# First batch of an attention and MoE kernel: query-major products in plain float32

## The chip, the cores and the metric

The kernel runs on one core of one Trainium2 chip. The metric is the device time of one execution in microseconds, the median of several runs. The engines are TensorE (PE; its loading of weights is PEld), VectorE (DVE), ScalarE (ACT), GpSimd (POOL) and SyncE (SP), which issues the DMAs here.

## What is computed

Causal attention mixed with a read from a memory, for 4 batches, 8 heads, 576 positions and 64 columns per head, and behind it two feed-forward stages over the 2304 tokens.

```python
scores = scale * np.matmul(q, k.transpose(0, 1, 3, 2))      # causal mask, softmax
local = np.matmul(a, v)
q_p = phi(q)                                  # where(x > 0, x, exp(x) - 1) + 1
mem_ret = np.einsum('bhsd,bhde->bhse', q_p, M_prev)
mem_norm = np.einsum('bhsd,bhd->bhs', q_p, z_prev)[..., None] + 1e-06
out = g * (mem_ret / mem_norm) + (1 - g) * local            # g = sigmoid(beta) per head
...
r = np.maximum(x @ w_in, 0.0); y = (s * (r * r) + b) @ w_out
z = (sigmoid(y @ w_gate) * (y @ w_val)) @ w_out2
```

## The kernel before

Nearly all products are split products: each float32 operand is rounded to the engine's shorter format (`F32R`) as a high half, the difference is the low half, and three products (high by high, low by high, high by low) are summed. So most tiles are written twice, by ScalarE the high half, by VectorE or GpSimd the low half.

**Stage one** is attention together with h, the product with `w_in`. Attention goes by pairs of heads, 16 pairs, four to a batch (`jobs`, line 356). For a pair, `plan_prep` loads and transposes k and q (tiles `KT`, `QT`) and makes phi(q), which is divided by its own norm on GpSimd (`phi_z`, `phi_s`, `phi_n`, lines 530 to 554), transposed (`ft`) and stacked as two halves (`FS`, line 429). The values and `M_prev` are split on GpSimd (`VHL`, `mst`). `plan_scores` has the scores with the queries on the partitions, in five tiles of 128 rows (the last holds 64 rows of both heads). VectorE takes the mask and the minimum (line 606), ScalarE the exponential with the row sum (line 668), VectorE 1/sum with 1 - g in it (line 676), and GpSimd divides P (`norm`, line 684). `plan_products` transposes P in 25 blocks of 128 x 128, splits them on the way out of PSUM (`p_hi`, `p_lo`, lines 776 and 780), and multiplies with the values as the stationary operand (lines 806 and 807) and the memory's part behind it (line 810): the result `acc` has the head's columns on the partitions and up to 320 queries along. It goes to `XB` (lines 830, 834), and when all four pairs of a batch are there, the batch's two windows, of 256 and 320 queries, are split into x (lines 891, 895). A group of h (`h_mm`, line 319) is 12 products of 256 or 320 columns: it needs the whole window of x and one of 16 tiles of `w_in`, which are made from float64 words on ScalarE, VectorE and GpSimd (lines 250 to 271).

**Later stages.** y, the product with `w_out` (line 1057), in 96 steps of 12 products, reads relu(h) back from DRAM. Then come the gated products in seven half-size products each (line 1294, tiles `m` and `set`) and the last product (line 1397), in three rounds. At the start of the first round, `w_out2` is made on the same engines.

**What sets the order.** Every piece of work is a task of `Plan` with an engine, a cost, a due time, what it reads and writes, and the buffers it takes. `Plan.order` goes through time and lets each engine that is free take the most urgent task that is ready. The tasks then stand in that order in each engine's queue, which runs in order. The due times come from the table `TUNE` (for instance `u + AT["pt"]` with u = 100 for each pair). Buffers that matter here: `s`, four PSUM banks; `VHL`, `QT`, `KT`, `mst` two each; `PTA`, `PTB` one.

```python
    chunks = [
        (*w, f + i) for f in range(0, NF, 2) for w in windows if w[0] == 0 for i in range(2)
    ]
    chunks += [(*w, f) for w in windows if w[0] for f in range(NF)]
```

The h groups of the first batch come first, two tiles of `w_in` at a time over both windows, then those of the other batches.

Of the kernel before, what the change touches and what calls it, by code (L numbers as in the profile page):

```python
# [150 lines left out]
def attention_moe_kernel(  # L151
# [18 lines left out]
    P = 128  # L170
# [192 lines left out]

    def load_consts2():
        for e in range(2):
            c = slice(e * NQ, e * NQ + NT4)
            nc.vector.tensor_copy(iom[:, :, c], iomg[:, e::2].unsqueeze(2).broadcast_to([P, NP, NT4]))
            r = slice(e * LAST, (e + 1) * LAST)
            nc.vector.tensor_copy(iom[r, :, NT4], iomg[r, e::2])

    def load_raw(j, src, dst, ta):
        b, p, t0, t1 = jobs[j]
        te = min(t1, NQ - 1)
        d4 = dst.rearrange("p t (h d) -> p t h d", h=2)
        for e in range(2):
            nc.sync.dma_start(
                d4[:, ta:te, e],
                src[b, 2 * p + e, ta * P : te * P].rearrange("(t p) d -> p t d", p=P),
            )
        if t1 == NQ and src is q:  # L380
            for e in range(2):
                nc.sync.dma_start(
                    d4[e * LAST : (e + 1) * LAST, NQ - 1, e], src[b, 2 * p + e, (NQ - 1) * P :]
                )
        elif t1 == NQ:
            lo = 0 if src is k else P - LAST
            nc.sync.dma_start(
                d4[lo : lo + LAST, NQ - 1],
                src[b, 2 * p : 2 * p + 2, (NQ - 1) * P :].rearrange("h p d -> p h d"),
            )  # L390

    def load_mem(j):
        b, p = jobs[j][:2]
        h = slice(2 * p, 2 * p + 2)
        raw = T["mraw", j] = at.tile([P, 2, D], F32, tag="mraw", name=f"mraw{j}", bufs=1)
        for i in range(2):
            nc.sync.dma_start(raw[i * D : (i + 1) * D], M_prev[b, h].rearrange("h d e -> d h e"))
        z = T["z", j] = at.tile([P, 2, D], F32, tag="zbc", name=f"zbc{j}", bufs=1)
# [20 lines left out]
    def bank(nt):  # L419
        return "s" if nt <= 4 else "w"  # L420
# [6 lines left out]
    def stack_lo(t, ds):  # L427
# [9 lines left out]
        "PTC": 1, "XB": 1, "x0": 1, f"x{SPLIT}": 1, "raw": 2, "f": FB, "wt": 16,  # L437
# [31 lines left out]
    def plan_prep(j):
# [276 lines left out]
    def plan_products(j):  # L746
# [138 lines left out]
        for win, (c0, n) in enumerate(((0, SPLIT), (SPLIT, BW))):  # L885
            if p == NP - 1 and (t0 == 0 if win == 0 else t1 == NQ):
# [26 lines left out]
    def plan_h(m):  # L913
# [619 lines left out]
```

## Time and profile before

| what | value |
|---|---|
| runs | 1090.73 us median of 3 (1089.75 to 1091.71) |
| profiled execution, its span | 1090.0 us (the page gives no other time of it; the median stands 0.7 us above) |
| busy shares | PE 95%, PEld 90%, DVE 70%, ACT 59%, POOL 55% |
| matrix products | 6496 |
| DMA | 145.95 MB, 134 GB/s mean |

The busy shares are averages over the whole span. The page also cuts the span into 40 slices; in those of the first 100 us TensorE's digits are lower than later and its granted clock is below full, and VectorE's are at 8 and 9. The rows below read that stretch, the stage behind it and one later stretch apart from each other.

### The profile page before, as it was taken

What the parts mean: (1) busy time and instruction counts of PE and PEld (TensorE: products, weight loads), DVE (VectorE), ACT (ScalarE), POOL (GpSimd) and SP (SyncE); (2) the same over time, 40 slices, a digit from 0 to 9 for tenths busy, and PEclk for the clock granted to TensorE, in tenths of its full rate; (3) what the DMA queues carried; (4) which work ended last, traced back from release to release, by engine and by line L of the source; (5) the groups of instructions that cost most, each with busy time, mean ns of one, the idle gap of its engine ahead of it and who ended that gap; (6) DMA issues with size and microseconds to landing.
All of it is one profiled execution on the core that took longest, in us unless ns stands there. A gap on an engine that the chain in (4) does not pass through costs nothing.

```text
span 1090.0 us, 18804 instructions
## 1 busy us (share of the span) xinstructions
PE 1040.3 (95%) x6496; PEld 977.0 (90%) x6496; DVE 766.3 (70%) x1434; ACT 647.6 (59%) x1407; POOL 598.4 (55%) x590
## 2 busy tenths in 40 slices
PE   4887998999999998999999999899999999999998
PEld 3676997899999998999999999898789998899986
DVE  5998987867667645777897765999726677266631
ACT  4877787787778656566666654565335453245421
POOL 5656666545434415474784554999427774177600
PEclk8877999999999999999999999999999999999999
DMA  5333554232323118868577776544214330133100
GB/s 135 80 82 81 170 145 120 72 85 81 106 85 92 47 61 264 259 204 267 174 245 262 261 268 221 183 160 160 87 63 136 113 125 29 63 119 118 69 24 35
DMA packets 135600, 145.95 MB, mean 134 GB/s; under 512 B 68176, under 2 KB 123472, under 8 KB 135504
## 3 DMA queue, kind: packets, MB, share of 16 engines
q1 hardware_dynamic: 135072, 144.74, 41.6%
q8 instruction: 51, 0.84, 0.3%
q14 instruction: 45, 0.37, 0.1%
q10 hardware_dynamic: 432, 0.01, 0.0%
HBM read 106.96 MB, written 37.75 MB: 133 GB/s over the span
## 4 chain that ended last, share of the span: by engine, by line
PE 80%; DVE 7%; POOL 7%; issue 2%; ACT 2%; DMA 1%; SPq 0%; DVEq 0%; POOLq 0%; ACTq 0%
PE m L1294 17%; PE h L319 17%; PE y L1057 16%; PE o L1397 14%; PE sc L626 3%; PE acc L806 3%; PE acc L807 2%; DVE set L1306 2%; PE pt_B L753 1%; PE sc L652 1%; POOL ws L1278 1%; POOL p L1316 1%; PE acc L810 1%; POOL w_out L271 1%; POOL P L684 1%
## 5 line engine op out<-in xcount | busy, mean ns | idle before, releaser
L1294 PE MATMUL m<-yt,ws 128*128 128x384 f32 x1512 | 264.5, 335 | 4.9 <-POOL ws L1278 3.5
L1294 PEld LDWEIGHTS m<-yt,ws 128*128 128x128 f32 x1512 | 262.0, 188 | 7.2 <-POOL ws L1278 4.7
L319 PE MATMUL h<-x,w_in 128*128 128x256 f32 (+1 forms) x1536 | 224.6, 300 | 5.5 <-POOL w_in L271 2.0
L319 PEld LDWEIGHTS h<-x,w_in 128*128 128x128 f32 x1536 | 207.8, 189 | 11.5 <-issue 3.7
L1306 DVE TENSOR_TENSOR set<-m,set 128x384 f32<-128x384 f32 x252 | 133.7, 554 | 57.8 <-PE m L1294 55.3
L1278 POOL TENSOR_TENSOR ws<-wf,ws 128x512 fp32r<-128x512 f32 (+1 forms) x108 | 124.7, 1175 | 86.4 <-ACT ws L1270 86.4
L1032 POOL TENSOR_SCALAR rr<-rr,sb_s,sb_b 128x384 f32<-128x384 f32 x96 | 103.8, 1088 | 96.7 <-ACT rr L1028 92.9
L1397 PE MATMUL o<-w_out,ps 128*128 128x512 f32 x648 | 154.0, 399 | 1.9 <-DVE ps L1387 1.5
L1397 PEld LDWEIGHTS o<-w_out,ps 128*128 128x128 f32 x648 | 122.7, 190 | 32.4 <-DVE ps L1387 2.3
L1057 PE MATMUL y<-gh,w_out 128*128 128x384 f32 x768 | 149.1, 335 | 2.4 <-ACT gh L1038 1.0
L1270 ACT CAST ws<-wf 128x512 fp32r<-128x512 f32 (+1 forms) x144 | 81.6, 568 | 103.4 <-PE m L1294 68.9
L1057 PEld LDWEIGHTS y<-gh,w_out 128*128 128x128 f32 x768 | 134.3, 188 | 3.3 <-ACT gh L1038 1.3
L1316 POOL TENSOR_TENSOR p<-set,set 128x384 f32<-128x384 f32 x72 | 85.7, 1214 | 40.9 <-DVE set L1306 40.9
L684 POOL TENSOR_SCALAR P<-P,rs 128x384 f32<-128x384 f32 (+3 forms) x144 | 85.2, 612 | 38.9 <-DVE rs L676 18.4
L1043 DVE TENSOR_TENSOR gl<-rr,gh 128x384 fp32r<-128x384 f32 x96 | 66.9, 701 | 51.5 <-PE y L1057 24.0
L606 DVE CUSTOM_DVE_ANT_0 P<-sc,mask 128x384 f32<-128x384 f32 (+2 forms) x144 | 70.5, 516 | 29.4 <-PE sc L626 13.6
L668 ACT ACTIVATE P<-P,nm 128x384 f32<-128x384 f32 (+2 forms) x144 | 83.8, 584 | 8.4 <-DVE nm L606 7.0
L329 ACT ACTIVATE r<-h 128x320 f32<-128x320 f32 (+1 forms) x128 | 52.3, 410 | 60.8 <-PE h L319 47.7
L1057 PE MATMUL y<-gl,w_out 128*128 128x384 f32 x384 | 82.0, 334 | 0.0
L1387 DVE TENSOR_TENSOR ps<-p,ps 128x512 fp32r<-128x512 f32 x54 | 47.4, 896 | 44.2 <-ACT ps L1374 44.2
L1374 ACT CAST ps<-p 128x512 fp32r<-128x512 f32 x54 | 32.5, 620 | 64.1 <-PE o L1397 50.6
L1038 ACT CAST gh<-rr 128x384 fp32r<-128x384 f32 x96 | 48.8, 511 | 33.2 <-PE y L1057 26.0
(134 smaller groups left out, 1712.1 us busy)
## 6 DMA issues: line engine op xcount, KB each, us to landing
wf<-weight_scratch SPq DMA_DIRECT2D x36, 896.0 KB, 4.5
rr<-relu_scratch SPq DMA_DIRECT2D x96, 192.0 KB, 3.7
raw_w_out<-in_moe_w_out_dram SPq DMA_DIRECT2D x28, 512.0 KB, 4.0
weight_scratch<-wm SPq DMA_DIRECT2D x12, 896.0 KB, 5.6
relu_scratch<-r SPq DMA_DIRECT2D x32, 320.0 KB, 2.3
raw_w_in<-in_moe_w_in_dram SPq DMA_DIRECT2D x16, 512.0 KB, 3.9
relu_scratch<-r SPq DMA_DIRECT2D x32, 256.0 KB, 2.3
raw_gv<-in_moe_w_gate_dram SPq DMA_DIRECT2D x12, 512.0 KB, 3.9
```

What stands on the lines that cost most here:

```text
L319: nc.tensor.matmul(t[:, :n], wt[:, wi, c], x[:, xi, c], start=(m == 0), stop=(m == 3 * NK - 1))
L606: nc.vector.tensor_tensor_reduce(out=pr, in0=ps, in1=mk, scale=1.0, scalar=3e38, op0=ALU.add, op1=ALU.min, accum_out=nm,)
L668: nc.scalar.activation(pr, pr, AF.Exp, bias=T.pop(("nm", j, e, t)), scale=-1.0, accum_out=T["sums", j][:, col : col + 1],)
L684: nc.gpsimd.tensor_scalar(out=pr, in0=pr, scalar1=T["rs", j, part][:, n : n + 1], scalar2=1.0, op0=ALU.mult, op1=ALU.mult,)
L1032: nc.gpsimd.tensor_scalar(out=r, in0=r, scalar1=sb_s, scalar2=sb_b, op0=ALU.mult, op1=ALU.add)
L1057: nc.tensor.matmul(accs[wi][d][:, :n], w_out_sb[f][:, x, d], y, start=(f == 0 and x == 0 and y is gh), stop=(f == NF - 1 and y is gl),)
L1270: nc.scalar.copy(t[:, 0, :m], flat(a, m))
L1278: engine[LOS[i]].tensor_tensor(out=t[:, 1, :m], in0=flat(a, m), in1=t[:, 0, :m].bitcast(F32), op=ALU.subtract)
L1294: nc.tensor.matmul(acc, wt[:, a, k : k + P], yt[:, y, c], start=(m == 0), stop=(m == 3 * K2 - 1),)
L1306: nc.vector.tensor_tensor(out=t[:, o], in0=Z["m", z, x], in1=t[:, i], op=ALU.add)
L1316: engine[TIMES[o]].tensor_tensor(out=p[:, f + HF * OF[o][0], OF[o][1]], in0=Z["set", z][:, o], in1=Z["set", zg][:, o], op=ALU.mult,)
L1397: nc.tensor.matmul(Z["zo", z], Z["ps", z, i][:, a, k * P : (k + 1) * P], w_out2_sb[f][:, x].rearrange("p c f -> p (c f)"), start=(i == k = ...
```

## The change

The four pairs of the first batch (`DIRECT`) take another path; the other twelve keep theirs.

- P is neither summed nor divided on its way. The exponentials are transposed as they are, copied out of PSUM once, in float32 (`p_copy`, on ScalarE, the last block on VectorE), and are now the stationary operand. The moving operand is the values, plain float32 with a column of ones beside them (65 columns, `load_vals`), so that the row sum comes with the product. The result has the queries on the partitions.
- phi is taken from the transposed q, so no second transpose is needed; its product with `M_prev`, with `z_prev` as the 65th column (`load_mem_f32`, `mem`), gives the norm too.
- Both results are divided as they leave PSUM (`mem_norm`, `norm`), added on GpSimd (`join`), transposed back (`xt`) and split into x at once, pair by pair (`x_hi`, `x_lo`). h of the first batch now needs these parts of all four pairs.
- The order of a pair's score tiles is rows 0 and 1, then 2, 3 and 4. `TUNE` has other due times for all tasks of the kernel, so the later stages are ordered anew too.

```diff
 TUNE = {
-    "lq": -580.2, "lk": -761.1, "lv": -464.9, "lm": 272.6, "q": -185.6, "k": -57.8, "phi": 44.8,
...
+    "mem": 39.5, "lq": -622.0, "lk": -752.9, "lv": -921.7, "lm": 533.7, "q": -351.0,
...
-ENG = {"split": "DVE"}
+ENG = {"split": "DVE", "join": "POOL"}
+EVICT = {"A0": "ACT", "A1": "ACT", "B0": "ACT", "B1": "ACT", "C0": "ACT", "C1": "ACT", "D": "DVE"}
...
+    DIRECT = range(NP)
...
+    def load_vals(j):
+        t = at.tile([P, NQ, 2, 2, D], F32, tag="VHL", name=f"vals{j}")
...
+        nc.gpsimd.memset(t[:, :, :, D], 1.0)
+        nc.gpsimd.memset(t[: P - LAST, NQ - 1], 0.0)
+
+    def load_mem_f32(j):
...
+        nc.sync.dma_start(t[:, :D], M_prev[b, h].rearrange("h d e -> (h d) e"))
+        nc.sync.dma_start(t[:, D : D + 1], z_prev[b, h].rearrange("h (d o) -> (h d) o", o=1))
...
+                        nc.tensor.matmul(
+                            both[e][1][:, i, : D + 1], f[r, t * P : (t + 1) * P], z[r, : D + 1],
+                            start=(i == 0), stop=(i == len(both[e][0]) - 1),
+                        )
...
+    UNITS = {
+        "A0": [(0, 0, 0), (0, 1, 0), (0, 1, P)],
+        "A1": [(1, 0, 0), (1, 1, 0), (1, 1, P)],
+        "B0": [(0, 2, k * P) for k in range(3)],
+        "B1": [(1, 2, k * P) for k in range(3)],
+        "C0": [(0, 3, k * P) for k in range(4)],
+        "C1": [(1, 3, k * P) for k in range(4)],
+        "D": [(0, 4, min(k * P, S - P)) for k in range(5)],
+    }
+    WINS = {0: ["A0", "A1"], 1: ["B0", "B1", "C0", "C1", "D"]}
...
+            if EVICT[g] == "ACT":
+                nc.scalar.copy(flat, ps)
+            else:
+                nc.vector.tensor_copy(flat, ps)
...
+                    for i, k in ks:
+                        nc.tensor.matmul(
+                            o[r, c, : D + 1], pt[:, i, n], vt[:, k, h, : D + 1],
+                            start=first,
...
+            nc.vector.scalar_tensor_tensor(
+                out=rs[:, :nu], in0=o[:, :, D], scalar=1e-9, in1=iomu[:, p, 4 * win : 4 * win + nu],
+                op0=ALU.add, op1=ALU.mult,
+            )
+            nc.vector.reciprocal(rs[:, :nu], rs[:, :nu])
+            nc.vector.tensor_tensor(
+                out=x[:, :nu], in0=o[:, :, :D],
+                in1=rs[:, :nu].unsqueeze(2).broadcast_to([P, nu, D]), op=ALU.mult,
+            )
...
+            nc.scalar.copy(xw[b, c0][:, 0, p], T["xt", j, win][:, :n])
...
             "PE", 12 * mm(n), lambda: h_mm(b, c0, n, f), u,
-            reads=[("x", b, c0), ("wt", f)] + ([("hc", m - 1)] if m else []),
+            reads=[("x", b, c0), ("wt", f)]
+            + ([("xb", b, int(c0 > 0), pp) for pp in range(NP)] if b * NP in DIRECT else []) + ([("hc", m - 1)] if m else []),
...
     for j in range(NJ):
+        if j in DIRECT:
+            prep_direct(j)
+            scores_direct(j)
+            products_direct(j)
+            continue
         plan_prep(j)
```

TensorE's queue, the products with the values in the start-up. Before, the fourth pair's first head, second window (`acc_1_0`; `VHL` are the split values, `FS` phi, `mst` the memory):

```order
L806 MATMUL acc_1_0_999<-PTB_880,VHL_541 128x320
L807 MATMUL acc_1_0_999<-PTB_880,VHL_541 64x320
L806 MATMUL acc_1_0_999<-PTB_880,VHL_541 128x320
L807 MATMUL acc_1_0_999<-PTB_880,VHL_541 64x320
L806 MATMUL acc_1_0_999<-PTB_880,VHL_541 128x320
L807 MATMUL acc_1_0_999<-PTB_880,VHL_541 64x320
L806 MATMUL acc_1_0_999<-PT_C,VHL_541 128x192
L807 MATMUL acc_1_0_999<-PT_C,VHL_541 64x192
L806 MATMUL acc_1_0_999<-PTB_880,VHL_541 128x64
L807 MATMUL acc_1_0_999<-PTB_880,VHL_541 64x64
L810 MATMUL acc_1_0_999<-FS_0_843,mst_556 128x320
```

After, the same place in the third pair (`o_1` is the second window's result, `vals` the values with ones):

```order
L443 MATMUL qt_883<-ident,rawq 128x128 x5
L1172 MATMUL pt_C_893<-ident,P_0_3_854 128x128 x4
L1172 MATMUL pt_C_906<-ident,P_1_3_880 128x128 x4
L1212 MATMUL o_1_805<-vals_464,PT_B 128x65 x8
L1212 MATMUL o_1_805<-vals_464,PT_B 64x65 x10
L1172 MATMUL pt_A_941<-ident,P_0_0_889 128x128
L1172 MATMUL pt_A_941<-ident,P_0_1_898 128x128 x2
L1172 MATMUL pt_A_953<-ident,P_1_0_903 128x128
L1172 MATMUL pt_A_953<-ident,P_1_1_911 128x128 x2
L443 MATMUL kt_957<-ident,rawk 128x128 x5
```

Eleven long products per head and window have become 30 short ones per pair, each with a block of P as its weights, and the next pair's transposes stand right behind them.

TensorE's queue, the first h group. Before, it stands behind the last product of the fourth pair, with the scores of the fifth pair done:

```order
L807 MATMUL acc_1_1_1298<-PTB_1169,VHL_802 64x64
L810 MATMUL acc_1_1_1298<-FS_1_1105,mst_817 128x256
L810 MATMUL acc_1_1_1298<-FS_1_1105,mst_817 128x64
L319 MATMUL h_0_0_1319<-x_0_1296,w_in_136 128x256 x12
L319 MATMUL h_0_1_1337<-x_0_1296,w_in_145 128x256 x12
```

After:

```order
L1246 MATMUL xt_0_1067<-ident,X_0_1019 128x128 x2
L1212 MATMUL o_1_1061<-vals_725,PT_B 128x65 x3
L1079 MATMUL sc_0_3_1076<-KT_703,QT_829 128x512
L1079 MATMUL sc_1_3_1077<-KT_703,QT_829 128x512
L1079 MATMUL sc_0_3_1076<-KT_703,QT_829 128x512
L1079 MATMUL sc_1_3_1077<-KT_703,QT_829 128x512
L1079 MATMUL sc_0_3_1076<-KT_703,QT_829 128x512
L1079 MATMUL sc_1_3_1077<-KT_703,QT_829 128x512
L1172 MATMUL pt_D<-ident,P_4_1057 128x128 x5
L321 MATMUL h_0_0_1096<-x_0_417,w_in_223 128x256 x12
L443 MATMUL kt_1119<-ident,rawk 128x128 x5
```

The first h group now stands in the middle of the fourth pair, behind the transposes of its first window (`xt_0`); its blocks C and most of its second window follow later. Further on in this queue, before, one y step of 12 products stands among the last h groups; after, some 15 steps do, with 12 or 24 h products between them.

VectorE's queue, twelve rows of one pair in the start-up. Before (`PTB`, `PT_A`, `PT_C` are low halves of P transposed, `XB` sums):

```order
L834 TENSOR_TENSOR XB_410<-acc_0_0_660,XB_410 64x256
L780 TENSOR_TENSOR PTB_619<-pt_B_671,PTB_619 128x384
L541 TENSOR_REDUCE nrm_708<-phit_666 128x10
L542 SCALAR_TENSOR_TENSOR nrm_708<-nrm_708,gt 128x10
L547 RECIPROCAL nrm_708<-nrm_708 128x10
L780 TENSOR_TENSOR PT_A_706<-pt_A_697,PT_A_706 128x384
L780 TENSOR_TENSOR PT_C<-pt_C,PT_C 128x384
L780 TENSOR_TENSOR PTB_619<-pt_D_712,PTB_619 128x2x256
L606 ISA P_1_3_734,nm_8_735<-sc_1_3_591,mask 128x512
L606 ISA nm_8_735 128x1
L834 TENSOR_TENSOR XB_410<-acc_0_1_723,XB_410 64x256
L780 TENSOR_TENSOR PTB_619<-pt_D_730,PTB_619 128x256
```

After (`ro`, `rm` are row factors, `X` the divided products, `MX` the memory's part):

```order
L1266 TENSOR_TENSOR x_256_506<-xt_1_770,x_256_506 128x320
L1225 SCALAR_TENSOR_TENSOR ro_0_796<-o_0_762,iomu 128x4
L1229 RECIPROCAL ro_0_796<-ro_0_796 128x4
L1230 TENSOR_TENSOR X_0_795<-o_0_762,ro_0_796 128x256
L255 TENSOR_SCALAR raw_w_in_622<-raw_w_in_622 128x512
L258 SCALAR_TENSOR_TENSOR raw_w_in_622<-raw_w_in_622 128x512
L1043 SCALAR_TENSOR_TENSOR rm_832<-ret_0_781,gtu 128x5
L1043 SCALAR_TENSOR_TENSOR rm_832<-ret_1_782,gtu 128x4
L1048 RECIPROCAL rm_832<-rm_832 128x9
L1051 TENSOR_TENSOR MX_831<-ret_0_781,rm_832 128x5x64
L1051 TENSOR_TENSOR MX_831<-ret_1_782,rm_832 128x4x64
L974 SCALAR_TENSOR_TENSOR QT_829<-qt_814,QT_829 128x640
```

The low halves of P are gone from this queue; the divisions and the low halves of x have come, and the making of `w_in` stands between as before.

## Rows read from the trace of the kernel before

**Rows 1.** Busy time by stretch: us, busy of each engine (instructions), PEclk, DMA share, GB/s

```profile
40.00:60.00 20.00, 16.52 (x101) 13.84 (x102) 18.11 (x46) 15.52 (x40) 13.15 (x16) 0.74 0.35 89
80.00:105.00 25.00, 19.93 (x128) 17.09 (x129) 22.43 (x50) 18.48 (x43) 13.31 (x17) 0.73 0.32 84
105.00:410.00 305.00, 298.27 (x2384) 283.63 (x2383) 222.86 (x544) 227.31 (x560) 148.38 (x186) 1.00 0.33 96
662.00:764.00 102.00, 95.52 (x529) 91.30 (x527) 94.70 (x136) 60.59 (x114) 91.09 (x70) 1.00 0.52 177
```

**Rows 2.** The tile x and the h products that read it: times, first and last start

```profile
L319 PE MATMUL h<-x,w_in x1536: 274/307/417, 104.9 to 462.6; 128*128 128x256 f32 x96, 128*128 128x320 f32 x96
...
  DVE x L895: 4.2, 2
```

**Rows 3.** Chain of waits, in order of time: start, us, what

```profile
47.24 1.13 PE pt_B L753 x4
...
67.70 1.13 PE pt_B L753 x4
```

**Rows 4.** VectorE's groups, first 470 us, removed for four pairs: busy, mean ns, idle before

```profile
L834 DVE TENSOR_TENSOR XB<-acc,XB 64x256 f32<-64x256 f32 (+2 forms) x80 | 29.7, 387 | 20.0 <-ACT XB L830 19.0
L780 DVE TENSOR_TENSOR PTB<-pt_B,PTB 128x384 fp32r<-128x384 f32 (+1 forms) x48 | 27.7, 592 | 4.9 <-ACT PTB L776 4.6
L780 DVE TENSOR_TENSOR PT_A<-pt_A,PT_A 128x384 fp32r<-128x384 f32 x32 | 17.6, 550 | 5.6 <-ACT PT_A L776 5.1
...
L780 DVE TENSOR_TENSOR PTB<-pt_D,PTB 128x512 fp32r<-128x512 f32 (+1 forms) x32 | 17.2, 549 | 1.1 <-ACT PTB L776 0.8
...
L429 DVE TENSOR_TENSOR FS<-ft,FS 64x640 fp32r<-64x640 f32 x16 | 13.1, 818 | 3.1 <-ACT FS L425 2.3
L541 DVE TENSOR_REDUCE nrm<-phit 128x10 f32<-128x640 f32 x16 | 13.0, 813 | 2.1 <-POOL phit L533 2.0
...
L895 DVE TENSOR_TENSOR x<-XB,x 128x1024 fp32r<-128x1024 f32 (+1 forms) x8 | 10.8, 1352 | 6.9 <-ACT x L891 6.8
...
L780 DVE TENSOR_TENSOR PT_C<-pt_C,PT_C 128x384 fp32r<-128x384 f32 x16 | 8.8, 551 | 0.1
...
L676 DVE SCALAR_TENSOR_TENSOR rs<-sums,iom 128x5 f32<-128x5 f32 (+1 forms) x32 | 7.3, 229 | 5.1 <-ACT P L668 4.8
```

**Rows 5.** The same view, a group that stays, used as a bound

```profile
L484 DVE SCALAR_TENSOR_TENSOR QT<-qt,QT 128x640 fp32r<-128x640 f32 x16 | 13.2, 822 | 5.4 <-ACT QT L480 5.3
```

**Rows 6.** Timeline of TensorE at clock 1.00: start, us, what

```profile
262.13 0.96 PE L626 MATMUL sc<-KT,QT 64*128 64x128 f32 x12
...
265.53 1.49 PE L626 MATMUL sc<-KT,QT 64*128 64x384 f32 x12
...
276.80 0.96 PE L652 MATMUL sc<-KT,QT 128*128 128x288 f32 x6
...
282.29 0.49 PE L753 MATMUL pt_C<-ident,P 128*128 128x128 f32 x3
282.62 0.60 PE L753 MATMUL pt_D<-ident,P 128*128 128x128 f32 x4
...
285.49 0.39 PE L806 MATMUL acc<-PTB,VHL 128*128 128x320 f32 x1
...
286.63 0.22 PE L806 MATMUL acc<-PTB,VHL 128*128 128x64 f32 x1
286.68 0.22 PE L807 MATMUL acc<-PTB,VHL 128*64 128x64 f32 x1
...
286.97 0.71 PE L416 MATMUL qt<-ident,rawq 128*128 128x128 f32 x5
```

**Rows 7.** Timeline of TensorE, the end of the first pair's scores

```profile
15.82 1.65 PE L626 MATMUL sc<-KT,QT 64*128 64x128 f32 x12
```

More of the change, by code (lines that the diff above doesn't have):

```diff
@@ L353, in attention_moe_kernel @@
     iom = at.tile([P, NP, NC], F32, name="iom", bufs=1)
+    iomu = at.tile([P, NP, NC], F32, name="iomu", bufs=1)
+    gtu = at.tile([P, NP, NC], F32, name="gtu", bufs=1)
+    VW = D + 2
     jobs = [(b, p, 0, NQ) for b in range(B) for p in range(NP)]
     NJ = len(jobs)
+    DIRECT = range(NP)
     W1 = 2 * BW
@@ L369, in load_consts2 @@
             nc.vector.tensor_copy(iom[r, :, NT4], iomg[r, e::2])
+            for dst, src in ((iomu, iomg), (gtu, gt)):
+                nc.vector.tensor_copy(
+                    dst[:, :, e : 2 * NT4 : 2], src[:, e::2].unsqueeze(2).broadcast_to([P, NP, NT4])
+                )
+                nc.vector.tensor_copy(dst[r, :, NC - 1], src[r, e::2])
     def load_raw(j, src, dst, ta):
@@ L373, in load_raw @@
         te = min(t1, NQ - 1)
-        d4 = dst.rearrange("p t (h d) -> p t h d", h=2)
+        d4 = dst if len(dst.shape) == 4 else dst.rearrange("p t (h d) -> p t h d", h=2)
         for e in range(2):
@@ L399, in load_mem @@
         nc.sync.dma_start(z, z_prev[b, h].partition_broadcast(P))
+    def load_vals(j):
+        t = at.tile([P, NQ, 2, 2, D], F32, tag="VHL", name=f"vals{j}")
+        t = T["v", j] = t.rearrange("p t h x d -> p (t h x d)")[:, : NQ * 2 * VW].rearrange(
+            "p (t h d) -> p t h d", h=2, d=VW
+        )
+        nc.gpsimd.memset(t[:, :, :, D], 1.0)
+        nc.gpsimd.memset(t[: P - LAST, NQ - 1], 0.0)
+    def load_mem_f32(j):
+        b, p = jobs[j][:2]
+        h = slice(2 * p, 2 * p + 2)
+        t = at.tile([P, 2, 2, D], F32, tag="mst", name=f"mem{j}")
+        t = T["m", j] = t.rearrange("p a b d -> p (a b d)")[:, :VW]
+        nc.sync.dma_start(t[:, :D], M_prev[b, h].rearrange("h d e -> (h d) e"))
+        nc.sync.dma_start(t[:, D : D + 1], z_prev[b, h].rearrange("h (d o) -> (h d) o", o=1))
     def prep_m(j):
@@ L436, in attention_moe_kernel @@
         "P1": 3, "P2": 3, "P3": 3, "P4": 1, "rs0": 2, "rs1": 2, "sums": 2, "PTA": 1, "PTB": 1,
-        "PTC": 1, "XB": 1, "x0": 1, f"x{SPLIT}": 1, "raw": 2, "f": FB, "wt": 16,
+        "PTC": 1, "XB": 1, "x0": 1, f"x{SPLIT}": 1, "X": 3, "MX": 2, "raw": 2, "f": FB, "wt": 16,
         "raw2": RAW2, "f2": FB, "w2": 16, "rr": RR, "gh": GG, "gl": GG, "yacc": 2,
@@ L447, in mm, with mm4 @@
         return max(108, 15 + n // 2.35)
+    def mm4(n):
+        return max(224, 15 + 1.75 * n)
     def act(n):
@@ L459, in plan_load @@
         u = 100 * j
+        direct = j in DIRECT
         for src, dst, ta, key, du in (
@@ L462, in plan_load @@
         ):
+            if src is v and direct:
+                add(
+                    "POOL", 400, lambda: load_vals(j), u + AT["lv"] - 10,
+                    new=[("VHL", ("v", j))],
+                )
+                add(
+                    "SP", 600 * ne, lambda: load_raw(j, v, T["v", j][:, :, :, :D], 0), u + du,
+                    writes=[("v", j)], late=1900, size=t1 * P * 800,
+                )
+                continue
             add(
@@ L466, in plan_load @@
             )
+        if direct:
+            add(
+                "SP", 1200, lambda: load_mem_f32(j), u + AT["lm"], new=[("mst", ("m", j))],
+                late=1900, size=1e5,
+            )
+            return
         add("SP", 1800, lambda: load_mem(j), u + AT["lm"], new=[("mem", ("mem", j))], late=1900, size=1e5)
@@ L1465, in attention_moe_kernel @@
     for j in range(NJ):
+        if j in DIRECT:
+            prep_direct(j)
+            scores_direct(j)
+            products_direct(j)
+            continue
         plan_prep(j)
```

301 lines of the change are left out of this document (added), and 11 rows, old and new, of the table TUNE.

## The prediction

> **What bounds the kernel now.** I read the busy shares by stretch first, because one average hides four different limits [rows 1]. From 40 to 105 us VectorE is busy 18.11 of 20 us and 22.43 of 25, that is 0.90, and TensorE runs at a mean granted clock of 0.73 to 0.74, a mixture of its two levels. From 105 to 410 us it turns round: TensorE is busy 298.27 of 305 us at clock 1.00, VectorE 222.86. From 662 to 764 us VectorE is the limit again, 94.70 of 102. Then I looked for where the first stage ends. The first product with w_in starts at 104.9 us [rows 2]. It can't start sooner, since it needs window 0 of the first batch for all four pairs, while every later pair has such products to lie beside. So the first 105 us are a start-up in which one engine works and the others wait for it, and what is saved there moves everything behind it. The chain of waits gives its beat: the transposes of the block pt_B of one pair start at 47.24 us, those of the next at 67.70, so a pair takes 20.46 us [rows 3]. After 105 us TensorE's work counts instead: each us of it added there is a us lost.
>
> The edit thus moves work from the engine that bounds the start-up to the one that will. The question is which of them is fuller afterwards.
>
> **What VectorE loses and gains, per pair.** Removed, from groups that hold all 16 pairs [rows 4]: the low halves of the transposed P (27.7 + 17.6 + 17.2 + 8.8 us), the sums into XB (29.7), the two stackings of phi (2 x 13.1), the sum over phi times z (13.0), the late split of x (10.8) and the small row factors (7.3, and some 12.7 for their reciprocals and the like for nrm, an estimate: four more tiny operations a pair at about 0.2). That is 71.3 + 29.7 + 26.2 + 13.0 + 10.8 + 20 = 171 us, or 10.7 per pair. Added: one copy of 640 columns (D), near the 640-column QT row of 0.82 [rows 5]; two normalisations, two of M and two low halves of x, each of 256 or 320 columns, 0.45 as the mean of nearly such shapes in the XB group (387 ns over its three forms) and the PT_A group (550 for 384 columns), so 2.7; seven tiny factors and reciprocals at 0.23, so 1.6. Together 5.1. From 20.46 x 0.90 = 18.5 us VectorE goes to 12.9 per pair.
>
> ScalarE loses as much (its high halves, stackings and accumulator reads go) and GpSimd loses the division of P, so neither comes near 13 us; I cost both at nothing while VectorE or TensorE needs more. The loads are cheaper by one DMA a pair, and the values now land straight in the tile the products read, behind a GpSimd memset. They are issued a pair ahead, so I cost them at nothing; without that cover one late load is worth the 5 us or so that a pair's first products would stand.
>
> **What TensorE gains, per pair.** At clock 1.00 [rows 6] three transposes take 0.33 us from start to start (282.29 to 282.62), 0.11 each. The score products of a pair take 0.96 + 1.49 + 0.96 less overlap, 3.2. The eleven split products of one head's second window run from 285.49 to 286.97, 1.48; the first window has 1024 columns where that has 2752, so 0.55; four of these per pair make 4.06. Before: 40 transposes x 0.11 + 3.2 + 4.06 = 11.7. After: kt, qt and the 25 of P are 35 transposes, 3.85; scores 3.2; the join's four transposes and two small products, 0.66; and 30 products with V plus 10 with M in plain float32, 40 times an unknown price c.
>
> No row shows c: every product in the trace is of split operands, and the only plain float32 on this engine are the transposes. Bounds: no less than a plain transpose, 0.11; no more than four of them, 0.44. I take 0.22: a split product of 64 columns costs 0.05 from start to start (286.63 to 286.68), and a plain one has to multiply two halves by two halves, four of those. So TensorE goes to 3.85 + 3.2 + 0.66 + 8.8 = 16.5 us per pair, 4.8 more, and passes VectorE's 12.9: it becomes the bound of the start-up, with VectorE at 0.78 of it.
>
> A rule speaks for the upper bound. The row first: a plain float32 transpose takes 0.11, a split product with as many stationary columns 0.05 [rows 6]. The Trainium skill's page TensorE: Matmul & The Clock Gate (section Weight-path perf modes) says that fast weight load, the quick way of filling the array, is not used for FP32; and FP8 and Floating Point Precision (TensorE Precision Notes) says that true FP32 takes four passes. If each pass loaded its weights the slow way, c would be 0.44, and the sum would come out slower, as in the first rival; by the split row it is 0.22.
>
> **The sum.** In the new order the transposes of P of the first pair stand where the first scores end, at 17.4 us in the trace (15.82 + 1.65) [rows 7]. From there to the first h stand four pairs, less what the first pair has done (4.3), less what of the fourth is left for later (8 transposes, 18 products with V, one join: 5.3), plus two sets of transposes of pair five (1.1): 66.0 - 4.3 - 5.3 + 1.1 = 57.5 us of TensorE. VectorE as bound was 0.90 busy; I take 0.85 for TensorE, since the first pair has nothing beside it. 57.5 / 0.85 = 67.6, so h starts at 85.0 instead of 104.9: **-19.9**.
>
> Against it: behind h's start TensorE now has the 5.3 of the fourth pair, and the part of pair five that before was done (kt, qt, ft and scores, 4.85, less the 1.1): 9.05 us, at the 0.98 busy of that stretch **+9.2**. At its start and once more h waited for the split of x, 4.2 us in all [rows 2]; x now comes pair by pair, so I take half of it back: **-2**. The other twelve pairs and the later stages have the same instructions, so **0**. The table of due times moves much in them, though: the first 14 or so y steps now stand between the last h groups, which is the same TensorE work in another order, and in 662 to 764 us VectorE keeps the same work, so its limit stays. Sum -12.7: the profiled span of 1090.0 becomes 1077.3. The median of the runs, 1090.73, stands 0.7 above that span, and I give **1078**.
>
> **The rivals.**
> - *The dear product* (slower). c decides alone. Before the first h stand 102 products with V and 40 with M, behind it 18: each ns of c costs 142 / 0.85 + 18 / 0.98 = 185 ns, so the 12.7 us are gone at c = 0.22 + 0.069 = 0.29 us. At 0.44 it is 0.22 x 185 = 41 us: +28, 1119; at 0.33, 1098. For it: the plain transpose at twice the split product. Against: no row has a float32 load per pass. Chance 0.11.
> - *The cheap product.* At c = 0.11 TensorE has 12.1 us per pair and VectorE's 12.9 binds: 3.6 pairs x 12.9 / 0.90 = 52, h at about 70, -34.9 + 7.2 - 2 = -30, so 1061. For it: a 65-column product moves half the columns of a transpose. Chance 0.13.
> - *The low clock stays.* TensorE ran at 0.73 from 40 to 105 us [rows 1]. Should that go on although it now has more to do, 57.5 us become 57.5 / 0.73 / 0.95 = 83, h starts at 100, -4.5 + 9.2 - 2: 1093. Against it: the clock is 1.00 wherever the rows show this engine busy above nine tenths. Halfway, 1085. Chance 0.10.
> - *The new order doesn't keep what it wins.* With y steps between the h groups each step needs a prepared w_out tile, VectorE, ScalarE and GpSimd in turn. A stall of 0.8 us at each of 14 steps takes back 11 us: 1089. Against: between the steps stand 12 or 24 h products, and VectorE is far from full there. Chance 0.07.
>
> **How the numbers follow.** The likeliest case, 0.59, spans 1068 to 1086 (0.92 or 0.78 in place of 0.85, and c within 0.03). Two in ten may lie outside the range: 1062 takes in nearly all of the cheap product, 1092 the clock and the order, and the dear product beyond 0.30 us is left out. About 0.2%, 2.2 us, is what a measurement of this kernel can tell from no change. Faster: 0.59 + 0.13 + half of the clock and order cases = 0.80. Same: 0.07, from these two. Slower: 0.11 of the dear product and 0.02 of the clock, 0.13.
>
> **What would show it.** In the profile after: first h between 80 and 90 us; VectorE below 0.8 busy in the stretch before it and TensorE above 0.85 at clock near 1.00; plain products at 0.2 to 0.23 us from start to start; a pair's beat of 18 to 19.5 us; last h some 13 us sooner than 462.6 once the y steps that then lie between are taken off. Wrong would be a first h after 95 us, products at 0.3 or more, a clock of 0.75 with TensorE full, or a first h on time with the gain lost between 400 and 760 us.

## The result, and the profile after

The changed kernel took **1077.9 us**, the median of 4 runs (1074.09 to 1079.14), against 1090.62 for the kernel before in the same comparison (4 runs, 1089.75 to 1091.71): a ratio of 0.9866 with a 95% interval of 0.9846 to 0.9887. The profiled execution took 1078.23 us, its span is 1076.4, so it is 13.6 us shorter than the span of 1090.0 before. On another chip the same kernel gave 1077.93 and a ratio of 0.9866 [0.9851, 0.9880] (beside the experiment that closes the hole, below).

Busy time by stretch, the view of [rows 1], in the changed kernel:

```profile
40.00:60.00 20.00, 18.35 (x167) 15.15 (x168) 15.42 (x44) 14.51 (x29) 7.13 (x9) 1.00 0.45 113
60.00:80.00 20.00, 19.37 (x165) 16.73 (x166) 15.20 (x41) 12.93 (x25) 7.15 (x6) 0.91 0.23 58
90.00:105.00 15.00, 11.97 (x71) 9.74 (x70) 12.81 (x35) 7.58 (x22) 13.04 (x15) 0.77 0.39 104
105.00:410.00 305.00, 300.62 (x2404) 287.40 (x2403) 217.65 (x519) 223.81 (x553) 140.21 (x176) 1.00 0.36 107
646.00:750.00 104.00, 95.90 (x529) 91.27 (x527) 95.95 (x134) 59.82 (x114) 88.00 (x69) 0.99 0.51 174
```

From 40 to 60 us the two engines have changed places: TensorE 18.35 of 20 at clock 1.00, VectorE 15.42, where [rows 1] had 16.52 at 0.74 and 18.11. The third row is a hole that the prediction didn't have: from 90 to 105 us TensorE is busy 11.97 of 15, at 0.77. The last row answers to 662 to 764 of before: as many instructions on TensorE (x529), 104 us long instead of 102.

The whole start-up, from the end of the first pair's scores to the first h:

```profile
16.50:79.20 62.70, 59.72 (x540) 51.07 (x538) 47.15 (x134) 44.50 (x86) 16.77 (x20) 0.97 0.42 103
```

The tile x and the h products that read it, as in [rows 2]:

```profile
L321 PE MATMUL h<-x,w_in x1536: 274/307/633, 79.2 to 475.1; 128*128 128x256 f32 x96, 128*128 128x320 f32 x96
...
  DVE x L942: 3.4, 2
```

The first h starts at 79.2 us instead of 104.9. The last one is later than before, at 475.1, because y steps now lie between. The wait for the split of x reads 3.4 us where it was 4.2. In both kernels that is one wait, counted for the weight load (1.8, before 2.2) and again for the matmul (1.6, before 2.0). TensorE's timeline shows it, before in the second window of the first batch, after in the second batch (L942):

```profile
110.47 1.73 PE L319 MATMUL h<-x,w_in 128*128 128x320 f32 x10 [1.98 <-DVE x L895]
```

```profile
197.04 1.45 PE L321 MATMUL h<-x,w_in 128*128 128x256 f32 x10 [1.61 <-DVE x L942]
```

The timeline of TensorE, two pairs of the start-up (start, us, what, idle before and its releaser):

```profile
16.48 1.48 PE L1172 MATMUL pt_A<-ident,P 128*128 128x128 f32 x6
...
20.46 0.78 PE L1212 MATMUL o<-vals,PT_B 128*128 128x65 f32 x6
21.17 1.07 PE L1079 MATMUL sc<-KT,QT 64*128 64x512 f32 x6
...
23.48 1.11 PE L1025 MATMUL ret<-mem,phi 64*128 64x65 f32 x16
24.52 0.33 PE L1031 MATMUL ret<-mem,phi 64*64 64x65 f32 x4
...
29.28 2.14 PE L1212 MATMUL o<-vals,PT_B 128*128 128x65 f32 x28
31.35 0.79 PE L1079 MATMUL sc<-KT,QT 64*128 64x384 f32 x6
...
32.67 0.49 PE L1172 MATMUL pt_A<-ident,P 128*128 128x128 f32 x3
...
50.06 0.88 PE L1172 MATMUL pt_A<-ident,P 128*128 128x128 f32 x6
```

The beat is 16.2 us for the first pair (16.48 to 32.67) and 17.4 for the second (to 50.06), against 20.46 in [rows 3]. The price that no row of the kernel before showed is here. Every plain product stands in the trace as two matmul instructions: x6 are three products, and they take 20.46 to 21.17, 0.24 us each. The group of x28 is four such products and ten of the last block, with 64 stationary columns: 2.07 less 4 x 0.24 leaves 0.11 for each of those. The eight products with `M_prev` (x16) take 23.48 to 24.52, 0.13 each. Over a pair that is 20 x 0.24 + 10 x 0.11 + 10 x 0.13 = 7.2 us, or 0.18 for each of the 40.

VectorE's added groups, first 470 us, for all four pairs (busy, mean ns, idle before):

```profile
L1230 DVE TENSOR_TENSOR X<-o,ro 128x256 f32<-128x256 f32 (+1 forms) x8 | 3.7, 458 | 0.3
L1266 DVE TENSOR_TENSOR x<-xt,x 128x256 fp32r<-128x256 f32 (+1 forms) x8 | 3.6, 453 | 2.7 <-ACT x L1261 2.6
...
L1191 DVE COPY PT_B<-pt_D 128x640 f32<-128x640 f32 x4 | 3.3, 824 | 0.5 <-PE pt_D L1172 0.4
L1051 DVE TENSOR_TENSOR MX<-ret,rm 128x320 f32<-128x320 f32 (+1 forms) x8 | 3.3, 453 | 0.1
L1229 DVE RECIPROCAL ro<-ro 128x4 f32<-128x4 f32 (+1 forms) x8 | 1.5, 184 | 0.3
L1225 DVE SCALAR_TENSOR_TENSOR ro<-o,iomu 128x4 f32<-128x4 f32 (+1 forms) x8 | 1.3, 157 | 5.9 <-PE o L1212 5.9
```

With the two groups of `rm` (0.9 each) they make 18.5 us, 4.6 per pair; the prediction had 5.1.

The hole at 90 us, first on TensorE and then on VectorE:

```profile
94.32 0.77 PE L443 MATMUL kt<-ident,rawk 128*128 128x128 f32 x5 [2.16 <-DVE nm L653]
95.96 0.41 PE L1246 MATMUL xt<-ident,X 128*128 128x128 f32 x2 [0.87 <-DVE nm L653]
...
98.47 3.57 PE L321 MATMUL h<-x,w_in 128*128 128x320 f32 x12
```

```profile
90.77 1.56 DVE L255 TENSOR_SCALAR raw_w_in<-raw_w_in 128x512 int32<-128x512 int32 x1
92.36 1.23 DVE L258 SCALAR_TENSOR_TENSOR raw_w_in<-raw_w_in 128x512 int32<-128x512 int32 x1
93.51 0.75 DVE L653 CUSTOM_DVE_ANT_0 P<-sc,mask 128x576 f32<-128x576 f32 x1
```

The transposes of k wait for the PSUM bank that the fifth pair's minimum reads. VectorE has that minimum in its queue behind 2.8 us of integer work on a w_in tile that nobody needs yet. Behind the hole the twelve h products take 3.57 us, twice what they take at full clock (the next 24 run from 103.45 to 106.76 us, 1.66 a dozen).

### The profile page after: what moved, and what is told of

Same layout as the page of the kernel before. It is cut to its first block, busy times and chain, and to the rows that moved or that the text cites. A ratio compares the mean times of both kernels' runs of the same rounds, so it can differ in the third digit from the quotient of the medians.

```text
span 1076.4 us, 19037 instructions
## 1 busy us (share of the span) xinstructions
PE 1043.2 (97%) x6696; PEld 981.2 (91%) x6696; DVE 741.1 (69%) x1408; ACT 623.8 (58%) x1341; POOL 560.9 (52%) x546
## 4 chain that ended last, share of the span: by engine, by line
PE 82%; DVE 8%; POOL 4%; ACT 2%; DMA 2%; issue 2%; SPq 0%; DVEq 0%; ACTq 0%; POOLq 0%
PE h L321 18%; PE m L1712 18%; PE y L1475 17%; PE o L1815 14%; PE sc L673 3%; DVE set L1724 2%; PE o L1212 2%; PE acc L854 1%; PE acc L853 1%; PE pt_B L800 1%; DVE raw_w_out L258 1%; POOL rr L1450 1%; PE kt L443 1%; PE acc L857 1%; PE sc L699 1%
## 5 line engine op out<-in xcount | busy, mean ns | idle before, releaser
L321 PE MATMUL h<-x,w_in 128*128 128x256 f32 (+1 forms) x1536 | 228.9, 301 | 1.9 <-DVE x L942 1.6
L321 PEld LDWEIGHTS h<-x,w_in 128*128 128x128 f32 x1536 | 210.0, 190 | 8.3 <-issue 3.2
L1450 POOL TENSOR_SCALAR rr<-rr,sb_s,sb_b 128x384 f32<-128x384 f32 x96 | 111.6, 1170 | 99.6 <-ACT rr L1446 87.0
L1461 DVE TENSOR_TENSOR gl<-rr,gh 128x384 fp32r<-128x384 f32 x96 | 69.4, 728 | 56.8 <-ACT gh L1456 31.9
L731 POOL TENSOR_SCALAR P<-P,rs 128x256 f32<-128x256 f32 (+4 forms) x108 | 62.7, 601 | 67.2 <-DVE rs L727 26.3
L653 DVE CUSTOM_DVE_ANT_0 P<-sc,mask 128x256 f32<-128x256 f32 (+4 forms) x144 | 69.9, 515 | 35.8 <-PE sc L673 13.8
L1475 PEld LDWEIGHTS y<-gl,w_out 128*128 128x128 f32 x384 | 67.8, 188 | 1.5 <-DVE gl L1461 1.5
L715 ACT ACTIVATE P<-P,nm 128x256 f32<-128x256 f32 (+4 forms) x108 | 62.9, 583 | 5.2 <-DVE nm L653 4.9
```

Of the source, the lines that this page charges most:

```text
L321: nc.tensor.matmul(t[:, :n], wt[:, wi, c], x[:, xi, c], start=(m == 0), stop=(m == 3 * NK - 1))
L653: nc.vector.tensor_tensor_reduce(out=pr, in0=ps, in1=mk, scale=1.0, scalar=3e38, op0=ALU.add, op1=ALU.min, accum_out=nm,)
L715: nc.scalar.activation(pr, pr, AF.Exp, bias=T.pop(("nm", j, e, t)), scale=-1.0, accum_out=T["sums", j][:, col : col + 1],)
L1450: nc.gpsimd.tensor_scalar(out=r, in0=r, scalar1=sb_s, scalar2=sb_b, op0=ALU.mult, op1=ALU.add)
L1461: nc.vector.tensor_tensor(out=gl, in0=r_sb.pop(step), in1=gs[step][0].bitcast(F32), op=ALU.subtract)
L1475: nc.tensor.matmul(accs[wi][d][:, :n], w_out_sb[f][:, x, d], y, start=(f == 0 and x == 0 and y is gh), stop=(f == NF - 1 and y is gl),)
```

## The experiments

**The table of due times alone.** All pairs go the old way.

```diff
-    DIRECT = range(NP)
+    DIRECT = range(0)
```

> The new table of due times, with no pair on the new path (DIRECT empty): all 16 pairs as before, the whole result is computed. Theory (the gain is the path's, not the order's): VectorE bounds the start-up as before, first h at 100 to 110 us against 79.2 in the changed kernel, and the time is 1088 to 1100. Rival (a good part of the gain is the new order of the later stages, which the table brings): at or below 1085.

Measured: 1101.62 us (1099.19 to 1105.45), ratio 1.0095 [1.0069, 1.0121], the first h at 107.1. From 40 to 60 us VectorE is busy 18.14 of 20, as in [rows 1], and TensorE 14.00. The new order brings nothing by itself; with all pairs on the old path it costs 10 us, slightly more than the theory allowed. The rival falls.

**The path alone.** The new path, with the table of before (and a "mem" entry, which that one lacks).

```diff
-    "mem": 39.5, "lq": -622.0, "lk": -752.9, ...
+    "mem": 39.5,
+    "lq": -580.2, "lk": -761.1, "lv": -464.9, ...
```

> The new path for the first four pairs with the table of due times of before; the whole result is computed. Theory (the path alone takes the work off VectorE and so moves the first h): first h at 78 to 86 us, later stages as long as before, 1074 to 1084. Rival (path and table only work together): the first h comes after 90 us, or the time is above 1086.

Measured: 1084.42 us (1080.80 to 1089.86), ratio 0.9932 [0.9913, 0.9950], the first h at 79.5. The start-up gains all of its 25 us with the old table too; the time comes out at the theory's upper edge, since more of the gain is lost again behind it:

```profile
90.00:105.00 15.00, 10.94 (x60) 8.45 (x57) 14.20 (x33) 10.80 (x26) 9.27 (x12) 0.77 0.44 119
```

```profile
160.00:210.00 50.00, 44.32 (x309) 39.05 (x307) 36.06 (x88) 33.65 (x84) 24.22 (x30) 0.90 0.27 76
```

There is a hole at the same place (the transposes of k stand 3.34 us from 92.9 us on, and here the view names no releaser), and a second one between 160 and 210 us, where the changed kernel has 46.54 busy at 1.00. So the path makes the gain (-7.4 us under the old table), and the table, worth +10 without the path, keeps 7 us more of it.

**More TensorE work.** Each product with the values twice.

```diff
-                    for i, k in ks:
+                    for i, k, y in [(i, k, y) for i, k in ks for y in range(2)]:
...
-                                  and i == ks[-1][0]),
+                                  and i == ks[-1][0] and y == 1),
```

> Every plain float32 product with the values is issued twice into the same sum (row sums double too, so the quotient is the same): 30 more products per pair of the first batch. By the trace of the changed kernel they cost TensorE 20 x 0.24 + 10 x 0.12 = 6.0 us per pair. Theory (TensorE now bounds the start-up): the first h some 20 us later, about 99 us, and the time +20 to +25, 1098 to 1103. Rival (VectorE still bounds it and TensorE's work lies beside): +5 or less, below 1083. If the second product of a block cost less than the first, because its weights are there already, the increase would be half, some +12.

Measured: 1094.44 us (1091.14 to 1096.63), ratio 1.0014 [0.9998, 1.0029], some 16 us above the changed kernel by the two ratios; the first h at 95.8.

```profile
L1212 PE MATMUL o<-vals,PT_B 128*128 128x65 f32 x224 | 27.5, 275 | 0.6 <-ACT PT_B L1189 0.6
...
L1212 PE MATMUL o<-vals,PT_A 128*128 128x65 f32 x96 | 12.2, 280 | 0.0
L1212 PE MATMUL o<-vals,PT_B 128*64 128x65 f32 x160 | 9.5, 224 | 0.0
```

Their busy time went from 26.2 (14.9 + 6.5 + 4.8) to 49.2, and the group that ran from 29.28 to 31.35 us, 2.07, takes 4.12 here (32.52 to 36.64): the second product of a block costs as much as the first. TensorE bounds, as the theory has it. The increase is 16 and not the 20 to 25 of the theory: up to the first h TensorE is busy 17.6 us longer (77.32 for 59.72), but waits less (2.0 us for 3.0), and it stays at clock 1.00 all the way to 105 us (mean 0.97 before the first h in the changed kernel).

**More VectorE work.** The low half of x four times.

```diff
-            t = xw[b, c0]
...
+            for _ in range(4):
+                nc.vector.tensor_tensor(
+                    out=t[:, 1, p], in0=ps[:, :n], in1=t[:, 0, p].bitcast(F32), op=ALU.subtract,
+                )
```

> The low half of x in the new path is written four times instead of once (the same values): by the trace of the changed kernel three times 0.42 + 0.49, 2.7 us more VectorE work per pair, 11 us for the batch, with no other engine's work changed. VectorE goes from 0.77 to some 0.92 of a pair's 17.4 us. Theory (TensorE bounds, VectorE has room): first h within 3 us of 79.2 and the time +0 to +4, 1078 to 1082. Rival (VectorE still bounds the start-up): +10 or so, 1088.

Measured: 1089.26 us (1086.12 to 1093.27), ratio 0.9981 [0.9964, 0.9997], some 12 us above the changed kernel; the first h at 91.0. My theory gave +0 to +4 and is wrong, and the rival's number came without its reason: between 16.5 and 91.0 us VectorE is busy only 54.53 of 74.5. Stretches of 5 us:

```profile
40.00:45.00 5.00, 3.86 (x31) 2.93 (x29) 4.50 (x12) 3.71 (x7) 2.41 (x2) 1.00 0.31 66
...
50.00:55.00 5.00, 5.00 (x30) 4.32 (x31) 1.71 (x5) 2.60 (x6) 0.00 (x0) 0.50 0.07 17
...
65.00:70.00 5.00, 2.94 (x16) 1.61 (x16) 4.83 (x12) 2.58 (x5) 0.74 (x1) 1.00 0.26 59
70.00:75.00 5.00, 4.97 (x33) 4.55 (x34) 3.75 (x13) 3.52 (x8) 0.00 (x0) 0.66 0.01 3
75.00:80.00 5.00, 5.00 (x35) 4.76 (x35) 1.14 (x4) 1.72 (x4) 2.35 (x3) 0.50 0.00 0
```

Where VectorE is full (4.50 and 4.83 of 5) TensorE has gaps, and behind the gaps it runs at 1.2 GHz: fully busy at 0.50. Then VectorE stands nearly idle. Up to the first h TensorE's gaps grow from 3.0 to 6.5 us and its busy time from 59.7 to 68.0 for the same 540 instructions: 3.5 + 8.3 = 11.8, which is the whole shift. Two of the gaps on TensorE's timeline:

```profile
45.51 0.29 PE L1079 MATMUL sc<-KT,QT 64*128 64x128 f32 x1 [1.13 <-DVE x L1267]
...
70.03 0.92 PE L1079 MATMUL sc<-KT,QT 64*128 64x128 f32 x11 [1.33 <-DVE x L1267]
```

In all, 3.1 us of the gaps are four waits of the scores for the repeated write of x itself, which holds one of the four banks of `s` longer; the changed kernel has no such wait. So a mean share of 0.77 was no room for 2.7 us per pair at this place. Whether as much work elsewhere in VectorE's queue costs as much was not tried.

**Less TensorE work.** The way on the other side.

```diff
-                    for i, k in ks:
+                    for i, k in ks[:1]:
...
```

> Of the products with the values only the first block of keys of each row tile is left in (10 of 30 per pair); the other 20 are left out, so the result is not the reference's. By the trace of the changed kernel that takes 12 x 0.24 + 8 x 0.12 = 3.8 us of TensorE per pair away, 15 in the first batch and 13 of it ahead of the first h; VectorE, ScalarE and GpSimd keep their work. VectorE has 13.4 us per pair there, TensorE would have some 13. Theory (TensorE alone bounds the start-up): first h at 66 to 70 us and -8 to -13 against the changed kernel. Rival (VectorE is close behind, or gaps bring the half clock): first h after 73 us, and -5 or less.

Measured: 1071.47 us (1069.84 to 1071.88), ratio 0.9801 [0.9768, 0.9834], 7 us below the changed kernel; the first h at 73.4. Of the 13 us ahead of the first h 5.8 came: TensorE's gaps there grew from 3.0 to 5.3 us, and its mean clock went from 0.97 to 0.94.

```profile
30.00:35.00 5.00, 5.00 (x24) 4.06 (x25) 3.40 (x15) 3.64 (x9) 2.39 (x4) 0.50 0.51 138
...
40.00:45.00 5.00, 3.79 (x33) 2.72 (x30) 4.93 (x13) 3.78 (x8) 2.41 (x2) 1.00 0.35 75
```

The 5 us at half clock in the first row cost 2.5 us, and in the second row VectorE is full. The first h is the rival's, the time lies between the two (-7 for -8 to -13 or -5), and both of the rival's reasons are in the rows. TensorE bounds the changed start-up, and VectorE is close behind.

**The price of a product.** Each product of 65 columns as two, of 33 and 32.

```diff
-                    for i, k in ks:
+                    for i, k, y in [(i, k, y) for i, k in ks for y in (0, 33)]:
+                        w = slice(y, y + 33 - y // 33)
...
-                            o[r, c, : D + 1], pt[:, i, n], vt[:, k, h, : D + 1],
+                            o[r, c, w], pt[:, i, n], vt[:, k, h, w],
...
```

> Each plain float32 product with the values (65 columns) issued as two, of 33 and 32 columns; the whole result is computed. Theory A (a plain product's price is set by loading the block of P as weights and hardly by its columns): each half costs as much as the whole, TensorE has 6 us more per pair, and the kernel goes like the one with every product issued twice: first h near 96 us and +15 against the changed kernel. Theory B (the price goes by columns): two halves cost as much as one whole, first h within 3 us of 79 and +0 to +3.

Measured: 1116.01 us, the median of three (1109.62 to 1117.59; a fourth, 1134.46, stands over 1.5% above them and isn't counted), ratio 1.0199 [1.0162, 1.0237], some 36 above the changed kernel on the same chip by the two ratios; the first h at 113.3. TensorE's timeline, and its stretches:

```profile
20.04 1.42 PE L1213 MATMUL o<-vals,PT_A 128*128 128x33 f32 x12
21.30 0.53 PE L1172 MATMUL pt_B<-ident,P 128*128 128x128 f32 x3
```

```profile
60.00:65.00 5.00, 5.00 (x51) 4.89 (x51) 1.37 (x6) 0.69 (x2) 0.32 (x2) 0.63 0.01 3
...
75.00:80.00 5.00, 5.00 (x25) 4.94 (x24) 1.20 (x3) 1.92 (x3) 0.72 (x1) 0.50 0.22 51
```

At full clock half a product takes 1.26 / 6 = 0.21 us, where the whole takes 0.24. Theory A's price holds: it goes by the block of weights and hardly by the columns that pass it. Its +15 doesn't, and the other half of the loss neither theory had (the run with every product twice had its first h at 95.8): the granted clock is at its lower level for long stretches in which TensorE is busy 5.00 of 5.00 us, without a gap.

**The hole closed.** In the list of tasks, one entry moves: the integer work of w_in tile 6 goes ahead of the fifth pair's low half of q (`made` keeps the tasks' numbers).

```diff
...
-        for n in plan.order():
+        seq = plan.order()
+        seq.remove(made["w_in6"])
+        seq.insert(seq.index(made["q", 5]), made["w_in6"])
+        for n in seq:
```

It ran on one chip with the changed kernel, with nothing edited, beside it.

> The changed kernel, nothing edited, on the chip on which the next three run. Expected: 1078 to 1080, 0.987 of the kernel before; first h at 79, and again two waits of TensorE between 91 and 96 us, 3.0 us in all, with the half clock behind them.

> The changed kernel with one VectorE task elsewhere: the two integer operations on one w_in tile (raw_w_in6), which stood ahead of the fifth pair's last minimum and held TensorE's next transposes of k from 92.15 to 94.32 us, now stand four instructions earlier, where VectorE waited 1.0 us for ScalarE. Nothing else is moved and the whole result is computed. Theory (a gap in TensorE's work costs its own length and a stretch at half clock behind it): 2.0 us of waiting go, and of the 3.3 us lost at half clock between 96.6 and 106 some or all, so -2 to -5 against the changed kernel. Rival (the gap is hidden or moves to the next wait): within 1 us.

Measured: the changed kernel 1077.93 us (1076.97 to 1078.97), 0.9866 [0.9851, 0.9880]; the edited one **1072.55** (1072.37 to 1074.12), 0.9821 [0.9805, 0.9837]. The changed kernel shows its two waits again, 2.16 and 0.87 us. The edited one takes 5.4 us less, and is faster than both kernels of this case. That is slightly more than the theory's -2 to -5, and far from the rival's 1 us. TensorE in the unedited kernel:

```profile
94.58 0.76 PE L443 MATMUL kt<-ident,rawk 128*128 128x128 f32 x5 [2.16 <-DVE nm L653]
...
105.56 0.49 PE L800 MATMUL pt_A<-ident,P 128*128 128x128 f32 x3
```

and in the edited one:

```profile
91.31 0.77 PE L443 MATMUL kt<-ident,rawk 128*128 128x128 f32 x5
93.14 0.41 PE L1246 MATMUL xt<-ident,X 128*128 128x128 f32 x2 [1.07 <-DVE nm L653]
...
101.13 0.49 PE L800 MATMUL pt_A<-ident,P 128*128 128x128 f32 x3
```

The two moved instructions, in their new place:

```profile
87.12 0.56 DVE L255 TENSOR_SCALAR raw_w_in<-raw_w_in 128x512 int32<-128x512 int32 x1
87.72 0.69 DVE L258 SCALAR_TENSOR_TENSOR raw_w_in<-raw_w_in 128x512 int32<-128x512 int32 x1
```

The wait of 2.16 us is gone, for two reasons that the run doesn't part: the two instructions stand sooner, and they are also shorter there, 1.25 us together for 2.8. The second wait stays (1.07 for 0.87). The clock from 90 to 105 us is 1.00, and the fifth pair's transposes of P (pt_A) start 4.4 us sooner; 1.2 of these were there at the first h already (78.2 for 79.4), ahead of the edit, since the stretch from 60 to 80 us ran at 1.00 here and at 0.91 there. Why that one stayed at full clock isn't settled. So 3.2 us of the gain stand at the hole itself, and 1.3 more come between 105 us and the first product m.

**The path for the second batch too.** The x of that batch goes through XB as before.

```diff
-    DIRECT = range(NP)
+    DIRECT = range(2 * NP)
...
```

> The second batch's four pairs on the new path too; its x is split from a sum in XB as before, and the whole result is computed. Theory (the path pays only where TensorE has no h products to lie beside; from 105 us on TensorE is 0.98 busy and bounds): by the trace of the changed kernel a pair on the new path costs TensorE about 15 us against 11.7, so 4 x 3.3 = +13 against the changed kernel, with VectorE less busy between 105 and 250 us. Rival (the path is better everywhere, since VectorE and ScalarE are relieved): equal or faster.

Measured: 1078.09 us (1076.64 to 1078.25), ratio 0.9864 [0.9849, 0.9879]: no difference from the changed kernel. TensorE between the first h and the first product m, here:

```profile
79.70:645.52 565.82, 563.97 (x4150) 546.90 (x4149) 380.43 (x800) 368.42 (x832) 261.82 (x267) 1.00 0.51 162
```

and in the kernel with the hole closed:

```profile
78.20:640.06 561.86, 554.54 (x3967) 536.91 (x3965) 410.36 (x844) 383.38 (x895) 301.30 (x309) 1.00 0.52 164
```

The four pairs do cost TensorE 9.4 us more than there (13 were expected), but its gaps fall to 1.9 us from 7.3, and from 8.5 in the changed kernel, which lost some more at half clock. VectorE has 30 us less to do, and neither wait of the hole at 90 us is left. So the theory has the cost right in kind and missed that the relief pays for it; of the rival's "equal or faster", equal is what came.

## Why the prediction came out right

The forecast of 1078 us is the time measured, and the direction and the mechanism hold. That it hits to 0.1 us is luck: the single terms were off in both directions and cancelled. Against the profile they are -25.7 for -19.9, +9.7 for +7.2, +2.4 for 0, which is -13.6 for -12.7; and the median stands 1.5 us above the span, not 0.7. Of the signs that were named, VectorE's and TensorE's busy shares (0.75 and 0.95) and the clock came. The first h (79.2 us, not 80 to 90), the beat (16.2 and 17.4, not 18 to 19.5) and the single products (0.24, 0.13 and 0.11, not 0.2 to 0.23) missed, all to the quick side but the 0.24. The last h at 475.1 has 14 more y steps ahead of it than before, 31.6 us of busy time, so without them it is some 19 us sooner instead of 13.

- **VectorE bounds the start-up and is relieved.** Right. It is busy 47.15 of the 62.7 us ahead of the first h, 0.75, or 13.1 us per beat of 17.4; forecast 12.9.
- **ScalarE comes nowhere near 13 us.** Wrong, though it cost nothing. It is busy 44.50 of the same 62.7 us, 12.3 per beat, nearly as full as VectorE: from 40 to 60 us its share fell only from 15.52 to 14.51 of 20 us, since the copies of P out of PSUM are mostly its work. GpSimd, with 4.7 per beat, is as free as forecast.
- **TensorE takes over with 16.5 us per pair.** Right in sum, 16.65 for the second pair (17.39 from 32.67 to 50.06, less 0.74 of waiting), and wrong in its parts, read from start to start over the same 17 us. The products cost 0.18 instead of c = 0.22, 7.3 us instead of 8.8. The rest was set too low: scores 3.7 instead of 3.2, 35 transposes 4.6 instead of 3.85, since they take 0.13 each in the mean (0.08 to 0.17 by group) and not 0.11, and the join 1.0 instead of 0.66.
- **57.5 us / 0.85.** This is the term that was mis-sized. From 16.5 us (forecast 17.4) to the first h are 62.7 us, in which TensorE is busy 59.72 at a mean clock of 0.97: 0.92 of full work, not 0.85. I had taken the first pair to stand alone; its gaps are short because kt and the next pair's scores fill them. So the first h came at 79.2 and not at 85.0.
- **+9.2 behind it, and -2 for h's wait.** Between the first h and the first m 9.7 us went back (104.9 to 661.70 before, 79.2 to 645.73 after):

```profile
104.90:661.70 556.80, 546.10 (x3882) 530.13 (x3881) 404.53 (x828) 381.73 (x884) 292.04 (x306) 1.00 0.52 163
```

```profile
79.20:645.73 566.53, 557.50 (x3967) 539.35 (x3966) 408.93 (x844) 382.86 (x895) 298.44 (x309) 0.99 0.52 163
```

TensorE is busy 11.4 us longer, and its gaps fall from 10.7 to 9.0. With the hole closed it is busy 8.4 us longer (554.54), which stands for the work left behind and is near the forecast's 9.05; the other 3.0 go with the lower clock of the changed kernel (0.99 for 1.00). The -2 was got from a wrong reading: the 4.2 us of [rows 2] are one wait of 2.0 us at 110.47, counted twice, and there was none at h's start. On TensorE the wait for x shrank by 0.4, from 2.0 to 1.6, and moved to the second batch; that all gaps together shrank by 1.7 is near the 2 by chance.
- **Later stages 0.** They lost 2.4 us, 1.7 of it between the first m and the first long run of the last product (102.6 before, 104.3 after), where the last product's wait for VectorE (`ps`) grew from 1.5 to 4.2 us.
- **The dear product** falls. A plain product costs 0.18 us in the mean and 0.24 at most. Its weight loads with 128 stationary columns take 191 to 192 ns each, those of a split h product 190. The Trainium skill's FP8 and Floating Point Precision (TensorE Precision Notes) has true FP32 take four passes; the trace shows two instructions per product, of 0.12 us each, and no run here shows four.
- **The cheap product** as a case of c = 0.11 falls as well, but its limit was tried with fewer products: the first h stops at 73.4 us, for VectorE is there.
- **The low clock stays** falls for the start-up (0.97) and came true for 90 to 105 us. It is the rival that I should have set in another place: not as a clock that doesn't rise, but as a gap with a bill behind it. VectorE at 0.78 of TensorE was the prediction's reading, and it came; that this leaves room was the expectation of the run with more VectorE work, and that run lost 12 us.
- **The new order** kept what it won: y's waits are 1.9 us in all, and the table alone and the path alone are both slower than the two together.

## What to carry to other kernels

Moving work from the bounding engine to one that waits pays until the second is full, but look for the moment when the two are level: here 6 us more of TensorE per pair cost 16 us in all and 2.7 us more of VectorE 12, and where VectorE's work held up TensorE, its gaps brought stretches at half clock with them. When a stage has been shortened, read the first stretch behind it for a new wait, and see what stands in the queue ahead of the instruction that is waited for: moving two instructions by four places took 3.2 us off at the spot, in a run that was 5.4 us faster, where the whole change brought 14.1 on that chip.

## What the runs showed of the hardware

- A plain float32 product with a block of P as weights is two instructions, 0.24 us together with 128 stationary columns, 0.11 with 64, 0.13 for a product with `M_prev` on 64 rows; halving the moving columns from 65 to 33 only brings 0.24 to 0.21. A second product with the same block costs as much as the first.
- TensorE's granted clock fell to its lower level behind gaps of 1 to 2 us (0.50 from 50 to 55 us with more VectorE work), but not behind each of them, and it also fell where the engine was busy 5.00 of 5.00 us with the short products of 33 columns (0.63 from 60 to 65 us, 0.50 from 75 to 80). A busy share near one doesn't show that the clock is there; the column beside it does.
- The integer operations on a w_in tile (L255, L258) took 1.56 and 1.23 us from 90.8 us on, and 0.57 and 0.69 from 81.4 on. Beside the slow pair GpSimd ran a 1.58 us subtraction on the values (L640), and so it did beside a slow L258 of 1.92 us at 68.9; whether that is the cause wasn't tried.
